# Three edits to the order of background work in a retention and two-layer MLP kernel

## The chip, the cores and the metric

The kernel runs on one core of a Trainium2 chip. Its engines work side by side, each through its own queue in order: TensorE (PE, matmuls into PSUM banks), VectorE (DVE), ScalarE (ACT), GpSimd (POOL), and SyncE (SP), which here only issues DMAs. The metric is the time of one execution on the device in microseconds (us), the median of several runs.

## What is computed

A retention layer over 4 batches, 8 heads, 768 steps and head size 64, then two MLPs on 3072 tokens of width 512 with a hidden width of 2048:

```python
def _attn_ref(q, k, v) -> np.ndarray:
    ...
    for t in range(S):
        state = gamma[None, :, None, None] * state + np.einsum('bhd,bhe->bhde', k[:, :, t], v[:, :, t])
        y[:, :, t] = scale * np.einsum('bhd,bhde->bhe', q[:, :, t], state)
    return y.astype(np.float32)
...
    h = x @ w_in
    g = np.maximum(0.01 * h, h)
    return (g @ w_out).astype(np.float32)
...
    h = x @ w_in
    g = h - np.tanh(h)
    return (g @ w_out).astype(np.float32)
```

The second MLP takes the first one's output. Weights and results keep more precision than one fp32r matmul gives: each operand is split into a high part (`xch`, `gh`, `wg`, rounded by ScalarE in `upper`) and a low part (`xcl`, `gl`, what is left, subtracted by VectorE in `lower`), and three matmuls (high x high, high x low, low x high) stand for one product.

## The kernel before

**Stages.** The retention comes first. Then the first MLP's input product runs as a stream of 168 products: the tokens go in three pairs of blocks (`sb`), and each of the 8 column groups `g` of a pair takes seven products P1 to P7 of 2 x 2 sub-blocks (the sums and differences of a fast matrix product) instead of eight. A product is six matmuls of 128x512. Its input forms of the activations are B11, B21, T1, T2, B22, T3 and T4, made in `build_xc` from the stored activations `x1s`; the weights' seven forms per group come from `form_sets`. Results are joined (`c`), rectified and stored in DRAM as `g1s`.

Then the outer steps: step `o` takes one 128-row piece of the hidden activations (loaded into `gr`, split into `gh` and `gl`) and adds its product with `w_out` to four PSUM banks, 12 matmuls a step, 16 steps for a block of 512 tokens. At the end of a block `evac` copies the four banks out on ScalarE (`st`, L692) and two ticks later they are stored in `x2s`. The first 48 outer steps (three blocks) run alone, in the loop over `ND_FROM`. After that the second MLP's input products (`Xd`, `Yd`, `Zd`, `prod`, 168 of them) are interleaved with the outer steps that are left, six matmuls in turn; a product's weight form `wf` is loaded from `wfs` four products ahead. The second MLP's own outer steps end the program. The blocks use banks 4 to 7, except that the second and the last use banks 0 to 3.

**Order of the work around it.** The order is written by hand: the program is emitted in one go, and `tick` counts emitted units of TensorE's work. Background work stands in queues of generators: `conv` converts the weights from float64 (`Convert`: load `raw`, one ScalarE step, four VectorE steps), `bg` and `forms` build weight forms, `bx` builds activation forms, `loads` loads activations. `run` takes from these queues as much work as a budget of estimated microseconds allows: 1.3 a product in the first stream, 1.85 an outer step in the loop over `ND_FROM`. A generator that yields `None` waits; `settle()` waits for the next tick. The converted second-layer weights become eight sets of forms (`form_d`); each set needs 16 free buffers before it starts, takes seven of them for its result, and `put_forms` stores them in `wfs` with seven DMAs, L299 and L301. A converted output weight is stored in `w2s` by `store2` (L271).

All SBUF buffers of this kind come from one pool of 94, first in, first out: `alloc` takes the one that was given back longest ago, and `give` returns a buffer as soon as its last reader is emitted. So the next writer of a buffer may have to wait for a DMA that still reads it. `defer(n, f)` puts off `f` by `n` ticks, and `flush` runs what is due, from the head of the list.

In the first stream `upper_g` and `lower_g` split the first outer activations around the last four products, and step 0 of the outer steps is emitted one product before the stream's end.

Of the kernel before, what the change touches and what calls it, by code (L numbers as in the profile page):

```python
# [14 lines left out]
AF = mybir.ActivationFunctionType  # L15
# [4 lines left out]
P = 128  # L20
NB, NH, NS, ND = 4, 8, 768, 64
# [4 lines left out]
NM = DFF // P  # L26
# [25 lines left out]
W2_EARLY, SLOT_US, W2_US, G_AHEAD = 8, 1.3, 1.2, 6  # L52
# [15 lines left out]
SPAN = 7 * NG  # L68

ND_FROM, N_TAIL, UNIT_US = 3 * NM, 28, 1.29  # L70
C_AHEAD, M_AHEAD, F_AHEAD, F_LOW, STORE_LAG = 6, 4, 4, 5, 3


@with_exitstack
def kernel(
# [12 lines left out]
    nc = tc.nc  # L88
# [13 lines left out]
    x2s = dr.tile([NC, NK, P, TB], F32, tag="x2s", name="x2s")  # L102
# [9 lines left out]
    def alloc(nm, dt=F32, shape=(P, TB)):  # L112
        pool, tag = free.popleft()
        serial[0] += 1
        t = pool.tile(list(shape), dt, tag=tag, name=f"{nm}_{serial[0]}")
        home[id(t)] = (t, pool, tag)
        return t

    def give(*ts):
        for t in ts:  # L120
            _, pool, tag = home.pop(id(t))
            free.append((pool, tag))
# [3 lines left out]
    now, tick = [-1], [0]  # L126

    def run(queues, us):

        while us > 0:  # L130
            for queue in queues:
                cost = next(queue[0], "end") if queue else None
                if cost is not None:
                    break
            if cost is None:
                return 0.0
            if cost == "end":
                queue.popleft()
            else:
                us -= cost  # L140
        return us

    def settle():

        t = tick[0]
        while tick[0] == t:
            yield None

    post = []

    def defer(n, f):
        post.append((tick[0] + n, f))

    def flush(all_=False):
        while post and (all_ or post[0][0] <= tick[0]):
            post.pop(0)[1]()

    def split(hi, lo, src, eng):

# [133 lines left out]
    forms = deque()  # L293
# [58 lines left out]
    one = Side(x1s, lambda sb, by: now[0] >= SPAN * sb - 7 + PROD[by][3])  # L352
# [19 lines left out]
    def build_xc(side, sb, part, done=None):  # L372
        while sb not in side.q:
            yield None
        q = side.q[sb]
        b11, b12, b21, b22 = q["B11"], q["B12"], q["B21"], q["B22"]

        def minus(eng, out, x, y):
            for kt in range(2):
                eng.tensor_tensor(out=out[kt], in0=x[kt], in1=y[kt], op=ALU.subtract)  # L380


        todo = (("B11", b11, "P1", None), ("B21", b21, "P2", (nc.vector, b11, b12, b11)), ("T1", b11, "P5", None),
                ("T2", b11, "P6", None), ("B22", b22, "P3", (nc.vector, b12, b22, b12)), ("T3", b12, "P7", None),
                ("T4", b21, "P4", None))
        for nm, src, by, nxt in todo[slice(*PARTS[part])]:
            while sb and not side.ready(sb, by):
                yield None
            if sb:
                for t2 in side.c[sb - 1].pop(nm):  # L390
                    give(*t2)
            while len(free) < 8:
                yield None
            if nm == "T2":
                minus(nc.vector, b11, b22, b11)
                yield 1.3
            if not sb and nm in ("T1", "T2"):
                yield from settle()
            out = [(alloc("xch", F32R), alloc("xcl", F32R)) for _ in range(2)]
            for kt in range(2):  # L400
                upper(out[kt][0], src[kt])
            yield from settle()
            for kt in range(2):
                lower(*out[kt], src[kt])
                yield 0.7
            side.c.setdefault(sb, {})[nm] = out
            if nxt:
                minus(*nxt)
                yield 1.3 if nxt[0] is nc.vector else 0.0
            if nm == "T3":  # L410
                minus(nc.vector, b21, b11, b21)
                yield 1.3
        if done:
            done()
# [7 lines left out]
    with tc.tile_pool(name="at", bufs=2, reuse_waits="tile") as at, \  # L422
# [168 lines left out]
        conv = deque([conversion(conv_in)])  # L591
        bg = deque([build_xc(one, 0, 0), build_wg(0), build_xc(one, 0, 1), build_wg(1), build_xc(one, 0, 2, free_x)])
        us = 0.0
# [12 lines left out]
        for s in range(len(steps)):  # L606
# [14 lines left out]
            if s >= CONV_FROM:  # L621
                us = run((conv, bg) if s % 2 else (bg, conv), min(us + ATT_US, ATT_US))
# [10 lines left out]
    NT = NC * NM  # L633
    GR, G, ACC, WE = {}, {}, {}, {}
# [9 lines left out]
    def load_g(o):  # L644
        if o < 2 * NT:
            nb, m = where_g(o)
            assert o < NT or (nb, m) in made2, (nb, m)
            GR[o] = alloc("gr")
            nc.sync.dma_start(out=GR[o], in_=(g1s if o < NT else g2s)[nb, m])  # L649

    def upper_g(o):
        if o < 2 * NT:
            G[o] = alloc("gh", F32R), None
            upper(G[o][0], GR[o])

    def lower_g(o):
        if o < 2 * NT:
            G[o] = G[o][0], alloc("gl", F32R)
            lower(*G[o], GR[o])
            give(GR.pop(o))  # L660
# [24 lines left out]
    def evac(o, half):  # L685
        if o % NM < NM - 1:
            return
        nb = where_g(o)[0]
        for j in (2 * half, 2 * half + 1):
            st = alloc("st")  # L690
            if o < NT:
                nc.scalar.activation(out=st.rearrange("p (a b) -> p a b", a=8),  # L692
                                     in_=ACC[j].rearrange("p (b a) -> p a b", a=8), func=AF.Copy)
                out_to = x2s[nb, j]
            else:
                if o == 2 * NT - 1 and j % 2:
                    nc.vector.tensor_copy(st, ACC[j])  # L697
                else:
                    nc.scalar.activation(out=st, in_=ACC[j], func=AF.Copy)
                r0 = j * NS + nb * P  # L700
                out_to = out[r0:r0 + P, :]

            def put(st=st, out_to=out_to):
                nc.sync.dma_start(out=out_to, in_=st)
                give(st)

            if o == 2 * NT - 1:
                put()
            else:
                defer(2, put)  # L710

    def step(o):
        for half in range(2):
# [72 lines left out]
    bx = deque(build_xc(one, sb, part) for sb in range(1, NSB) for part in range(3))  # L786
    loads = deque(load_xq(one, sb, lambda at=SPAN * (sb - 1) + 38: now[0] >= at) for sb in range(1, NSB))
    xleft = [(c, p) for c in range(2, NC) for p in range(NPAIR)]
    us = 0.0
    for i, (at_, sb, g, nm) in enumerate(stream):  # L790
        an, bn, bk, _ = PROD[nm]
        while g not in WG or bn not in XC.get(sb, {}):
            tick[0] += 1
            run((loads, bg, bx, conv), 0.01)
        product(sb, g, nm)
        now[0] = at_
        tick[0] += 1
        done, late[:] = late[:], []
        used = collect(sb, g, nm)
        for args in done:  # L800
            rectify(*args)
        if sb == NSB - 1 and nm == "P4":
            give(*WG[g][1])
        if xleft:
            c, p = xleft.pop(0)
            t = xw.pop((c, p))
            nc.sync.dma_start(out=x1s[c, p], in_=t)
            give(t)
        us = run((loads, conv, bg, bx) if not sb and at_ >= BG_FIRST and at_ % 2 == 0 else (loads, bg, bx, conv), min(us + SLOT_US - used, SLOT_US))
        if len(stream) - 8 <= i < len(stream) - 8 + G_AHEAD:  # L810
            load_g(i - len(stream) + 8)
        if len(stream) - 4 <= i < len(stream) - 1:
            upper_g(i - len(stream) + 4)
        if len(stream) - 3 <= i < len(stream) - 1:
            lower_g(i - len(stream) + 3)
        if i == len(stream) - 2:
            step(0)
    for t2 in XC[NSB - 1].values():
# [51 lines left out]
    def load_x0():  # L870
        q = {}
        for nm, kh, th in (("B11", 0, 0), ("B21", 1, 0), ("B12", 0, 1), ("B22", 1, 1)):
            while at_n[0] < (th + 1) * NM + 1:
                yield None
            q[nm] = [alloc("xq") for _ in range(2)]
            for i in range(2):
                nc.sync.dma_start(out=q[nm][i], in_=x2s[th, 2 * kh + i])
        arrive = tick[0] + LOAD_LEAD
        yield 0.0
        while tick[0] < arrive:  # L880
            yield None
        two.q[0] = q
# [7 lines left out]
    for n in range(ND_FROM):  # L890
        load_g(n + C_AHEAD if n + C_AHEAD < ND_FROM + M_AHEAD else 2 * NT)
        if n == 0:
            upper_g(3)
            lower_g(2)
            continue
        while n % NM not in WO:
            tick[0] += 1
            run((conv,), 0.01)
        step(n)
        at_n[0] = n  # L900
        upper_g(n + 3)
        lower_g(n + 2)
        if ND_FROM - F_AHEAD <= n:
            load_f(n - ND_FROM + F_AHEAD)
        tick[0] += 2
        flush()
        us = run((loads, bx, forms, conv), min(us + 1.85, 1.9))


    events = {}  # L910
# [266 lines left out]
```

## Time and profile before

| | us |
|---|---|
| median of 3 runs | 1083.74 |
| lowest and highest run | 1082.7 and 1086.09 |
| the profiled execution | 1087.43 |
| its span, first to last instruction | 1085.7 |
| PE busy in the span | 1056.3 (97%) |
| DVE busy in the span | 824.1 (76%) |
| ACT busy in the span | 702.6 (65%) |

Busy time is the time in which an engine had at least one instruction in work; matmuls are pipelined, so a busy TensorE starts a 128x512 matmul every 0.215 us although one lasts 0.38 us. The shares are means over very different stages: what a stage loses is seen in a view of that stage alone.

### The profile page before, as it was taken

What the parts mean: (1) busy time and instruction counts of PE and PEld (TensorE: products, weight loads), DVE (VectorE), ACT (ScalarE), POOL (GpSimd) and SP (SyncE); (2) the same over time, 40 slices, a digit from 0 to 9 for tenths busy, and PEclk for the clock granted to TensorE, in tenths of its full rate; (3) what the DMA queues carried; (4) which work ended last, traced back from release to release, by engine and by line L of the source; (5) the groups of instructions that cost most, each with busy time, mean ns of one, the idle gap of its engine ahead of it and who ended that gap; (6) DMA issues with size and microseconds to landing.
All of it is one profiled execution on the core that took longest, in us unless ns stands there. A gap on an engine that the chain in (4) does not pass through costs nothing. (4 is left out here: it accounts for less than half of the span.)

```text
span 1085.7 us, 17570 instructions
## 1 busy us (share of the span) xinstructions
PE 1056.3 (97%) x5931; PEld 912.6 (84%) x5931; DVE 824.1 (76%) x1363; ACT 702.6 (65%) x1251; POOL 91.5 (8%) x124
## 2 busy tenths in 40 slices
PE   9999889999999999999999889999999999999998
PEld 6888778888888888888888778888888888888887
DVE  3578887675787968978888679989788988767730
ACT  4666576665676546656677478978668866676530
POOL 3231000000000000001110000111011011101000
PEclk9999999999999999999999989999999999999999
DMA  9997465485467869969997998999998888887641
GB/s 226 261 259 194 142 228 194 159 286 215 174 233 262 281 233 387 388 242 289 306 291 243 285 309 282 265 287 276 274 305 235 246 256 247 250 245 221 201 146 39
DMA packets 208634, 267.67 MB, mean 247 GB/s; under 512 B 65056, under 2 KB 106144, under 8 KB 208544
## 3 DMA queue, kind: packets, MB, share of 16 engines
q1 hardware_dynamic: 197888, 247.52, 68.5%
q0 software_dynamic: 10368, 18.88, 10.1%
q8 instruction: 47, 0.77, 0.3%
q14 instruction: 43, 0.35, 0.1%
q10 hardware_dynamic: 288, 0.15, 0.0%
HBM read 161.63 MB, written 85.98 MB: 228 GB/s over the span
## 5 line engine op out<-in xcount | busy, mean ns | idle before, releaser
L679 PE MATMUL o<-gh,wo 128*128 128x512 f32 x768 | 241.6, 382 | 1.8 <-ACT st L692 1.8
L169 ACT ACTIVATE gh<-gr 128x512 fp32r<-128x512 f32 x192 | 118.0, 623 | 78.3 <-DMA gr<-g1s 37.1
L679 PEld LDWEIGHTS o<-gh,wo 128*128 128x128 f32 x768 | 146.3, 191 | 23.1 <-ACT st L692 2.2
L679 PE MATMUL o<-gl,wo 128*128 128x512 f32 x384 | 147.2, 383 | 8.4 <-DVE gl L175 8.3
L175 DVE TENSOR_TENSOR gl<-gr,gh 128x512 fp32r<-128x512 f32 x192 | 130.2, 685 | 26.9 <-ACT gh L169 23.4
L679 PE MATMUL o<-w2h,gl 128*128 128x512 f32 x384 | 145.5, 379 | 0.0
L679 PE MATMUL o<-w2h,gh 128*128 128x512 f32 x384 | 145.5, 379 | 0.0
L679 PE MATMUL o<-w2l,gh 128*128 128x512 f32 x384 | 145.5, 379 | 0.0
L1018 PE MATMUL Xd<-xch,wf 128*128 128x512 f32 x384 | 130.9, 383 | 3.8 <-ACT kp L920 3.8
L998 POOL DMA_DIRECT2D et<-h x72 | 62.0, 862 | 855.6 <-DMA wf<-wfs 415.5
L746 PE MATMUL X<-xch,wg 128*128 128x512 f32 x384 | 123.5, 381 | 4.1 <-DVE wg L175 1.8
L985 DVE COPY_PREDICATED es<-mk,et 128x512 f32<-128x512 uint16 x96 | 71.1, 744 | 46.6 <-ACT mk L959 46.5
L679 PEld LDWEIGHTS o<-gl,wo 128*128 128x128 f32 x384 | 73.2, 191 | 21.1 <-DVE gl L175 10.7
L746 PEld LDWEIGHTS X<-xch,wg 128*128 128x128 f32 x384 | 72.4, 189 | 16.9 <-DVE wg L175 2.6
L1018 PEld LDWEIGHTS Xd<-xch,wf 128*128 128x128 f32 x384 | 73.4, 191 | 14.8 <-ACT kp L920 4.2
L679 PEld LDWEIGHTS o<-w2h,gh 128*128 128x128 f32 x384 | 72.6, 189 | 10.3
L679 PEld LDWEIGHTS o<-w2l,gh 128*128 128x128 f32 x384 | 72.6, 189 | 10.3
L679 PEld LDWEIGHTS o<-w2h,gl 128*128 128x128 f32 x384 | 72.6, 189 | 10.3
L947 ACT ACTIVATE eu<-h 128x512 f32<-128x512 f32 x96 | 59.8, 623 | 28.6 <-DVE h L927 24.2
L746 PE MATMUL X<-xcl,wg 128*128 128x512 f32 x192 | 73.2, 381 | 1.5 <-DVE xcl L175 1.4
L963 DVE SCALAR_TENSOR_TENSOR ew<-eu,h 128x512 f32<-128x512 f32 x96 | 65.8, 685 | 10.5 <-ACT eu L947 4.6
L1018 PE MATMUL Xd<-xcl,wf 128*128 128x512 f32 x192 | 73.4, 382 | 0.0
(100 smaller groups left out, 2028.4 us busy)
## 6 DMA issues: line engine op xcount, KB each, us to landing
wf<-wfs SPq DMA_DIRECT2D x168, 256.0 KB, 4.4
g1s<-c SPq DMA_DIRECT2D x96, 256.0 KB, 2.1
gr<-g1s SPq DMA_DIRECT2D x96, 256.0 KB, 5.5
g2s<-es SPq DMA_DIRECT2D x96, 256.0 KB, 3.6
gr<-g2s SPq DMA_DIRECT2D x96, 256.0 KB, 4.1
et<-h POOLq DMA_DIRECT2D x72, 256.0 KB, 5.5
raw<-in_moe_w_in_dram SPq DMA_DIRECT2D x32, 512.0 KB, 5.8
raw<-in_moe_w_out_dram SPq DMA_DIRECT2D x32, 512.0 KB, 4.7
```

What stands on the lines that cost most here:

```text
L169: nc.scalar.activation(out=hi, in_=src, func=AF.Copy)
L175: nc.vector.tensor_tensor(out=lo, in0=src, in1=hi.bitcast(F32), op=ALU.subtract)
L679: nc.tensor.matmul(ACC[j], a, il(b), start=first and i == 0, stop=last and i == 2)
L746: nc.tensor.matmul(ps, w[:, c], il(x), start=first and kt == 0 and i == 0, stop=kt == 1 and i == 2, skip_group_check=True)
L947: nc.scalar.activation(out=e["u"], in_=h, func=AF.Square)
L963: nc.vector.scalar_tensor_tensor(out=e["w"], in0=e["u"], scalar=C3, in1=h, op0=ALU.mult, op1=ALU.mult)
L985: nc.vector.copy_predicated(out=e["s"], mask=e["mk"].bitcast(mybir.dt.uint16), data=e["th"])
L998: nc.gpsimd.dma_start(out=e["th"], in_=h, accum_op=ALU.add)
L1018: nc.tensor.matmul(ps, a, il(b), start=nm in ("P1", "P2", "P5") and kt == 0 and j == 0, stop=kt == 1 and j == 2, skip_group_check=True)
```

## The change

Four things. The first two blocks' results (outer steps 15 and 31) are copied out of PSUM with a delay of five ticks, that is after the third step behind the block's last has been emitted, and with them their stores and the loads that read them back (three steps later). `flush` runs whatever is due, wherever it stands in the list. The budget of an outer step in the loop over `ND_FROM` goes from 1.85 to 2.0. In the stream, the first outer activations are loaded three products earlier, and rounded and subtracted two products earlier. In `build_xc`, the first MLP's forms no longer wait for the next tick between rounding and subtracting.

```diff
-C_AHEAD, M_AHEAD, F_AHEAD, F_LOW, STORE_LAG = 6, 4, 4, 5, 3
+C_AHEAD, M_AHEAD, F_AHEAD, F_LOW, STORE_LAG, EVAC_LAG = 6, 4, 4, 5, 3, 5
...
     def flush(all_=False):
-        while post and (all_ or post[0][0] <= tick[0]):
-            post.pop(0)[1]()
+        while post:
+            due = [x for x in post if all_ or x[0] <= tick[0]]
+            if not due:
+                return
+            for x in due:
+                post.remove(x)
+                x[1]()
...
             for kt in range(2):
                 upper(out[kt][0], src[kt])
-            yield from settle()
+            yield 0.0
+            if side is not one:
+                yield from settle()
             for kt in range(2):
                 lower(*out[kt], src[kt])
                 yield 0.7
...
         nb = where_g(o)[0]
-        for j in (2 * half, 2 * half + 1):
...
+        js = (2 * half, 2 * half + 1)
+        if o < 2 * NM:
+            for j in js:
+                defer(EVAC_LAG, lambda j=j, acc=ACC[j]: take_out(o, nb, j, acc))
+        else:
+            for j in js:
+                take_out(o, nb, j, ACC[j])
+
+    def take_out(o, nb, j, acc):
+        st = alloc("st")
...
-        if len(stream) - 8 <= i < len(stream) - 8 + G_AHEAD:
-            load_g(i - len(stream) + 8)
-        if len(stream) - 4 <= i < len(stream) - 1:
-            upper_g(i - len(stream) + 4)
-        if len(stream) - 3 <= i < len(stream) - 1:
-            lower_g(i - len(stream) + 3)
+        if len(stream) - 11 <= i < len(stream) - 11 + G_AHEAD:
+            load_g(i - len(stream) + 11)
+        if len(stream) - 6 <= i < len(stream) - 3:
+            upper_g(i - len(stream) + 6)
+        if len(stream) - 5 <= i < len(stream) - 3:
+            lower_g(i - len(stream) + 5)
...
-            while at_n[0] < (th + 1) * NM + 1:
+            while at_n[0] < (th + 1) * NM + 4:
...
-        us = run((loads, bx, forms, conv), min(us + 1.85, 1.9))
+        us = run((loads, bx, forms, conv), min(us + 2.0, 2.0))
```

`take_out` is the old body of the loop in `evac`. TensorE's and GpSimd's instructions stand in the same order before and after. Line numbers after `flush` move by 5 to 15.

On SP, shortly after the loads of the second pair's activations (`xq_B`) for the second MLP, the last set of weight forms was stored (L299, L301; `wf` loads a form, `gr` an outer activation):

```order
L364 DMA xq_B_6701<-x2s 128x2x512
L649 DMA gr_6710<-g1s 128x512
L991 DMA g2s<-es_6613 128x512
L864 DMA wf_6745<-wfs 128x512
L649 DMA gr_6749<-g1s 128x512
L864 DMA wf_6769<-wfs 128x512
L864 DMA wf_6799<-wfs 128x512
L299 DMA wfs<-wg_6682 128x2x256
...
L301 DMA wfs<-wg_6688 128x512
L649 DMA gr_6813<-g1s 128x512
```

In the changed kernel no form store stands behind the same loads:

```order
L369 DMA xq_B_6707<-x2s 128x2x512
L879 DMA wf_6716<-wfs 128x512
L656 DMA gr_6726<-g1s 128x512
L1006 DMA g2s<-es_6641 128x512
L879 DMA wf_6762<-wfs 128x512
L656 DMA gr_6767<-g1s 128x512
L879 DMA wf_6788<-wfs 128x512
L879 DMA wf_6814<-wfs 128x512
L656 DMA gr_6824<-g1s 128x512
```

The last set stands some 100 rows further up in SP's queue, among the loads for the second MLP's first products:

```order
L202 DMA raw_1_5581<-in_moe_w_out_dram 128x1024
L276 DMA w2s<-cv_5459 128x512
L879 DMA wf_5591<-wfs 128x512
L879 DMA wf_5626<-wfs 128x512
L656 DMA gr_5634<-g1s 128x512
L304 DMA wfs<-wg_5506 128x2x256
...
L306 DMA wfs<-wg_5512 128x512
L879 DMA wf_5675<-wfs 128x512
```

So the store of the eighth set, behind 47 loads of `wf` before, stands behind 12 of them now.

On VectorE, at the turn from the second token pair to the third in the first stream (`c` joins two products of group `g` of the old pair, the number behind X, Y or Z being `g`; `xcl` is the low half of an activation form of the new pair, the third pair of them that of T1), there stood:

```order
L759 TENSOR_TENSOR c_3194<-Z_7_3187,P_280_3185 128x512
L759 TENSOR_TENSOR c_3213<-X_6_3106,P_275_3133 128x512
L175 TENSOR_TENSOR xcl_3216<-xq_B_3104,xch_3215 128x512
L175 TENSOR_TENSOR xcl_3218<-xq_B_3104,xch_3217 128x512
L759 TENSOR_TENSOR c_3239<-Y_7_3196,P_288_3227 128x512
L175 TENSOR_TENSOR xcl_3242<-xq_B_3124,xch_3241 128x512
L175 TENSOR_TENSOR xcl_3244<-xq_B_3124,xch_3243 128x512
L380 TENSOR_TENSOR xq_B_3104<-xq_B_3145,xq_B_3104 128x512 x2
L759 TENSOR_TENSOR c_3278<-Z_0_3271,P_295_3267 128x512
L175 TENSOR_TENSOR xcl_3281<-xq_B_3104,xch_3280 128x512
L175 TENSOR_TENSOR xcl_3283<-xq_B_3104,xch_3282 128x512
```

and now:

```order
L774 TENSOR_TENSOR c_3165<-Y_6_3128,P_277_3155 128x512
L180 TENSOR_TENSOR xcl_3188<-xq_B_3075,xch_3187 128x512
L180 TENSOR_TENSOR xcl_3190<-xq_B_3075,xch_3189 128x512
L774 TENSOR_TENSOR c_3202<-Z_7_3195,P_280_3185 128x512
L180 TENSOR_TENSOR xcl_3205<-xq_B_3095,xch_3204 128x512
L180 TENSOR_TENSOR xcl_3207<-xq_B_3095,xch_3206 128x512
L385 TENSOR_TENSOR xq_B_3075<-xq_B_3117,xq_B_3075 128x512 x2
L774 TENSOR_TENSOR c_3231<-X_6_3108,P_275_3135 128x512
L180 TENSOR_TENSOR xcl_3244<-xq_B_3075,xch_3243 128x512
L180 TENSOR_TENSOR xcl_3246<-xq_B_3075,xch_3245 128x512
```

T1's pair stood behind the first join of the new pair (Z_0) and now stands two joins of the old pair earlier, behind X_6.

On VectorE, at the end of the first stream, the first outer activation's low half (`gl`) stood behind the last group's second join (Y_7), with a converted weight's split (`wo`) just ahead of it:

```order
L759 TENSOR_TENSOR c_3975<-Y_7_3922,P_405_3959 128x512
L212 SCALAR_TENSOR_TENSOR cv_3916<-raw_1_3851,cv_3916 128x512
L215 SCALAR_TENSOR_TENSOR cv_3916<-raw_1_3851,cv_3916 128x512
L175 TENSOR_TENSOR wo_3997<-cv_3916,wo_3996 128x512
L175 TENSOR_TENSOR gl_4004<-gr_3920,gh_3980 128x512
L759 TENSOR_TENSOR c_4012<-X_7_3898,P_399_3929 128x512
```

and now:

```order
L217 SCALAR_TENSOR_TENSOR cv_3887<-raw_1_3823,cv_3887 128x512
L220 SCALAR_TENSOR_TENSOR cv_3887<-raw_1_3823,cv_3887 128x512
L774 TENSOR_TENSOR c_3961<-X_6_3814,P_388_3849 128x512
L180 TENSOR_TENSOR wo_3966<-cv_3887,wo_3965 128x512
L180 TENSOR_TENSOR gl_3985<-gr_3891,gh_3971 128x512
L774 TENSOR_TENSOR c_3993<-Y_7_3940,P_412_3979 128x512
```

It moved ahead of the join of Y_7 and of one weight unit's last steps.

## Rows read from the trace of the kernel before

**Rows 1.** Stretches: length; busy PE, PEld, DVE, ACT, POOL; clock, DMA share, GB/s.

```profile
116.00:160.00 44.00, 38.38 (x168) 30.56 (x167) 40.85 (x79) 30.32 (x56) 0.00 (x0) 1.00 0.65 221
...
352.00:474.00 122.00, 122.00 (x567) 106.81 (x567) 101.81 (x180) 67.33 (x117) 0.00 (x0) 1.00 0.86 302
420.00:460.00 40.00, 40.00 (x187) 35.02 (x186) 38.04 (x69) 25.44 (x46) 0.00 (x0) 1.00 1.07 388
...
596.00:640.00 44.00, 36.06 (x145) 29.95 (x145) 29.67 (x49) 24.63 (x46) 3.90 (x5) 0.88 0.87 287
640.00:1080.00 440.00, 440.00 (x2041) 385.29 (x2040) 333.34 (x524) 299.53 (x528) 45.13 (x53) 1.00 0.80 239
776.00:792.00 16.00, 16.00 (x76) 14.01 (x75) 11.38 (x18) 10.33 (x20) 0.86 (x1) 1.00 1.00 347
```

**Rows 2.** ACT's and DVE's longest waits, 352 to 474 us: total, times, longest.

```profile
ACT st L692 <- PE o L679: 15.2, 3, 7.1
DVE wg L175 <- ACT wg L169: 10.3, 3, 8.2
```

**Rows 3.** TensorE's waits, 116 to 160 us.

```profile
PE X L746 <- DVE wg L175: 1.8, 2, 1.2
PE Y L746 <- DVE xcl L175: 1.8, 1, 1.8
...
PE X L746 <- DVE xcl L175: 0.5, 1, 0.5
PE X L746 <- ACT xch L169: 0.4, 1, 0.4
```

**Rows 4.** TensorE's waits, 160 to 300 us.

```profile
PE Y L746 <- DVE xcl L175: 1.0, 1, 1.0
PE X L746 <- ACT xch L169: 0.9, 2, 0.5
PE X L746 <- DVE xcl L175: 0.9, 2, 0.5
```

**Rows 5.** Timeline of TensorE: start, us, instruction, idle before and its releaser.

```profile
346.75 0.48 PE L679 MATMUL o<-gl,wo 128*128 128x512 f32 x1 [1.82 <-DVE gl L175]
617.41 0.80 PE L679 MATMUL o<-gl,wo 128*128 128x512 f32 x1 [3.80 <-DVE gl L175]
631.80 0.79 PE L1018 MATMUL Xd<-xch,wf 128*128 128x512 f32 x1 [3.80 <-ACT kp L920]
```

**Rows 6.** TensorE's waits, 474 to 596 us.

```profile
PE o L679 <- DVE gl L175: 2.7, 2, 1.7
PE o L679 <- ACT st L692: 1.8, 1, 1.8
```

**Rows 7.** Chain that ended last, 590 to 640 us: start, us, what.

```profile
598.53 0.43 SPq L364
...
600.58 6.64 DMA g2s<-es
...
607.28 7.61 DMA wf<-wfs
...
623.18 5.72 DMA gr<-g1s
```

**Rows 8.** SP's waits, 596 to 632 us; the third row 486 to 504.

```profile
SPq L271 <- DVE cv L215: 5.6, 1, 5.6
SPq L864 <- DVE wg L177: 5.4, 1, 5.4
...
SPq L864 <- DMA wfs<-wg: 5.0, 1, 5.0
```

**Rows 9.** Timeline of SP: start, us, the form stores issued in a row.

```profile
617.15 4.61 SPq L299 DMA_DIRECT2D wfs<-wg  x6
```

**Rows 10.** Timelines of ScalarE and VectorE, as in rows 5.

```profile
611.07 0.63 ACT L169 ACTIVATE gh<-gr 128x512 fp32r<-128x512 f32 x1 [7.47 <-DMA g2s<-es]
...
499.92 0.69 DVE L963 SCALAR_TENSOR_TENSOR ew<-eu,h 128x512 f32<-128x512 f32 x1 [1.43 <-DMA wfs<-wg]
```

More of the change, by code (lines that the diff above doesn't have):

```diff
@@ L688, in evac, with put @@
         nb = where_g(o)[0]
-        for j in (2 * half, 2 * half + 1):
[L690 to L694, printed above, removed]
-            else:
[L696 to L710, printed above, removed]
+        js = (2 * half, 2 * half + 1)
[7 more added lines that the diff above has]
+        st = alloc("st")
+        if o < NT:
+            nc.scalar.activation(out=st.rearrange("p (a b) -> p a b", a=8),
+                                 in_=acc.rearrange("p (b a) -> p a b", a=8), func=AF.Copy)
+            out_to = x2s[nb, j]
+        else:
+            if o == 2 * NT - 1 and j % 2:
+                nc.vector.tensor_copy(st, acc)
+            else:
+                nc.scalar.activation(out=st, in_=acc, func=AF.Copy)
+            r0 = j * NS + nb * P
+            out_to = out[r0:r0 + P, :]
+        def put(st=st, out_to=out_to):
+            nc.sync.dma_start(out=out_to, in_=st)
+            give(st)
+        if o == 2 * NT - 1:
+            put()
+        else:
+            defer(2, put)
     def step(o):
```

## Prediction

> **What bounds the kernel now.** I read first the busy time by stretches. TensorE has the same 4320 large matmuls to run whatever the other engines do, so a gain can only come from stretches where it does not run them back to back. From 352 to 474 us, the first outer steps, it is busy for 122.00 of 122 us and starts 567 matmuls, 0.2152 us each (2.58 us for an outer step of 12); from 640 to 1080 us it is busy for all 440 [rows 1]. So the block ends inside 352 to 474 us cost TensorE nothing, although ScalarE stands there for 15.2 us in three waits (up to 7.1) for TensorE's last step before it can copy a block out, and VectorE waits 10.3 us for ScalarE [rows 2]: both run far enough ahead. The losses lie elsewhere, and the waits of TensorE name who was late:
> - 116 to 160 us: 5.6 us idle [rows 1], behind splits of the first activations (1.8, 0.5 and 0.4 us) and behind weight sets (1.8) [rows 3].
> - 160 to 300 us: 1.0 + 0.9 + 0.9 = 2.8 us, all behind the splits for the second and third token pair [rows 4].
> - 346.75 us: 1.82 us behind the first `gl`, the low half of the first outer activation [rows 5].
> - 474 to 596 us: 2.7 + 1.8 = 4.5 us [rows 6].
> - 596 to 640 us: the largest. 44 us hold 44/122 x 567 = 204 matmuls, 145 ran; 59 x 0.2152 = 12.8 us are lost. Of these 7.9 are idle (44 - 36.06), mostly two waits of 3.80 us [rows 1, 5]; the other 4.9 are matmuls run at a mean granted clock of 0.88, the two levels being 1.2 and 2.4 GHz.
>
> **Why 596 to 640 us stalls.** The chain of waits goes through DMAs: a store of `es` takes 6.64 us to release a buffer, a load of `wf` 7.61, and later a load of `gr` 5.72 [rows 7]. Two things meet there. Four loads of the next activations, 512 KB each, flood the DMA engines from 598.53 us on [rows 7]; and the last of the eight sets of second-layer weight forms is only now being built, because its builder asks for 16 free buffers and the pool has long been nearly empty. SP takes its queue in order, so it stood 5.6 us before a store of a converted weight and 5.4 us before a buffer that the last form's VectorE subtraction had to release; then it issued seven form stores in a row from 617.15 us, and the `gr` load behind them came at 623.18 [rows 7 to 9]. ScalarE waited 7.47 us for its activation meanwhile [rows 10].
>
> **The change, part by part**, against the profiled execution's own 1087.43 us (span 1085.7). TensorE's and GpSimd's programs are the same before and after, so each term is a wait.
>
> (1) More background work per outer step (2.0 instead of 1.85). By the code's own order, 5 of the 8 form sets were stored before the second layer's first product, and now 7 with it; the last set's stores stood behind the 47th `wf` load and now stand behind the 12th. Between the four big loads at 598 us and the next block end no form or conversion is left on SP, and on VectorE and ScalarE the eight steps of the last set go away from there. What is late next? The four big loads stay. Their twin, for the third token pair, is in the trace: 776 to 792 us, 347 GB/s, DMA share 1.00, and TensorE is busy for 16.00 of 16 us [rows 1]. There no form set is under way; that is what after will look like. Bounds for this term: 0 and -12.8. I take **-12.0**, by the twin.
>
> Its price: the last set now lands near 495 us. Where the seventh did, just before that, SP waited 5.0 us for form stores to release a buffer, and VectorE 1.43 us in one of three such waits; TensorE lost 1.0 (2.7 less the 1.7 of a later one) [rows 6, 8, 10]. The same set of waits comes a little later with the pool as empty or emptier. Bounds: -1.0 (the old wait goes and no new one comes) and +5.0 (SP's wait lands whole on TensorE). I take **+1.0**, nearer to what a set cost in the same stretch.
>
> VectorE's load in the outer stage: 38.04 of 40 us busy at 420 to 460 [rows 1]. 40 us are 15.5 steps, 0.15 more each is 2.3 us: 40.3, just full. Cover: it runs ahead of TensorE, as the waits for TensorE show. Cost 0; if the cover were gone, some 0.3 us per 40 us, below 1 us in the stage.
>
> (2) Copies of the first two blocks three steps later. ScalarE no longer waits at those two ends (at the third it still does, that copy is not deferred). TensorE waited for none of it: 0. Banks: the next user of the first block's banks is a block (16 steps) away, so no wait is added. The second block's stores and the loads that read them move three steps as well, 7.7 us, and the splits of the second layer's first activations with them; they are still emitted ahead of the products that read them, the tightest by some 30 matmuls (6.5 us). Cost 0, +1 if VectorE is late there.
>
> (3) First outer activations loaded, rounded and split two or three products earlier (a product is 6 x 0.2152 = 1.29 us). The first `gl` moves ahead by two products, 2.6 us, with a weight split just ahead of it as before; the wait was 1.82. **-1.8**, bounds 0 and -1.8.
>
> (4) Splits of the first layer without the pause of a product between rounding and subtracting. For the second and third pair the splits now stand up to four products before their use, where the first waits were for those emitted at the use itself: **-2.8**, bounds -1.4 and -2.8. In 116 to 160 us VectorE is busy for 40.85 of 44 us [rows 1], so there work has to go, not only move: by the order some 3 us of conversion steps move out of the first 120 matmuls. The 0.5 and 0.4 go, since the last split moves ahead by three products; of the 1.8 behind weight sets and the 0.9 us not shown I take half; the 1.8 of the first wait stays, since four conversion steps are still ahead of the second half of that split. Together **-2.0**, bounds +1 and -3.8.
>
> (5) The other 3.5 us of 474 to 596 us: one wait is a block end (1.8), unchanged; one hung on late loads (1.7), with one or two weight units fewer in work. **-0.6**, bounds +3 and -3.5.
>
> Sum: -12.0 + 1.0 - 1.8 - 2.8 - 2.0 - 0.6 = -18.2; 1087.43 - 18.2 = 1069.2. The profiled execution is 3.7 above the median of the three timed runs (1083.74) and 1.3 above the highest. If all of that is the profiler's, the median becomes 1065.5; if it is a deeper stall at 596 us than usual, there is 3.7 less to win there, and it becomes 1069.2. I take the middle, **1067**.
>
> **Rivals.**
> (a) The big loads alone hold the stall: for it, they are what fills the DMA queues in the chain; against it, the twin at 776 us. Only half of 12.8 goes: 1067 + 6 = 1073.
> (b) The outer stage becomes bound by DMA: one form set more (7 x 256 KB) and the loads of its two weight units (2 x 512 KB) have to pass before 474 us, 2.8 MB; the stretch 420 to 460 us already moves 388 GB/s at a share of 1.07 [rows 1]. At that rate 2.8 MB are 7.3 us, and if the lead of the splits covers only 2 of them, 5 reach TensorE: 1072. Against it: 352 to 474 us as a whole moves 302 GB/s. The Trainium skill, DMA: Bandwidth & Descriptors, section Specifications, gives about 358 GB/s as one core's share of HBM; by that the stretch could not run as it does, and 2.8 MB would be 7.8 us, an estimate from that page. The row's 388 is above it, so the measured rate decides.
> (c) Slower: the stall is not removed but doubled near 480 to 510 us. The form sets at the second layer's start drain the pool to a few buffers; if each `wf`, `gr` and `ew` then takes a buffer whose form store is unfinished, both sets there cost what the one at 596 us did: +2 x 12.8 - 18.2 = +7.4, so 1091 by the median. It decides once TensorE's new waits between 474 and 520 us pass some 18 us. Against it: two sets were stored in that stretch before and cost 1.0.
> (d) The change does nothing measurable: earlier sets only trade one wait for another of equal size, 1084.
>
> **How the numbers follow.** Forecast 0.76 (1058 to 1072), (a) 0.09, (b) 0.06, (c) 0.05, (d) 0.04. Low end: all bounds at their best are -12.8 - 1.0 - 1.8 - 2.8 - 3.8 - 3.5 = -25.7, 1058 by the median. High end: (a) with the +5.0 of the new place instead of +1.0, 1077. Range 1058 to 1078. A measurement of this kernel can tell about 0.3% (3.3 us) from no change: faster 0.88, same 0.06, slower 0.06 (of (c), and 0.01 of all else).
>
> **What would show it.** In the trace after: no wait of 3 us or more of TensorE between 590 and 640 us and no stretch there below full clock (1); at most 2 us of waits around 490 to 510 us (1); no wait before the first `gl` near 340 us (3); none behind `xcl` or `xch` between 160 and 300 us (4); ScalarE's wait for TensorE at the first two block ends gone with no time won (2). I am wrong if TensorE waits inside 352 to 470 us, if a new wait near 500 us is longer than 6 us, or if the stall at 600 us returns with the four big loads alone.

## The result and the profile after

| | before | after |
|---|---|---|
| median of 4 runs, us | 1083.64 | 1064.57 |
| lowest and highest, us | 1082.7 and 1086.09 | 1063.71 and 1066.49 |
| the profiled execution, us | 1087.43 | 1064.45 |
| its span, us | 1085.7 | 1062.7 |

The ratio is 0.9823, 95% interval 0.9802 to 0.9844: 19.1 us faster. 1067 was forecast, in a range of 1058 to 1078. The busy times by stretches of after, with the columns of [rows 1]:

```profile
116.00:160.00 44.00, 40.24 (x183) 33.81 (x182) 39.79 (x74) 31.96 (x58) 0.00 (x0) 1.00 0.64 227
160.00:300.00 140.00, 138.07 (x636) 119.39 (x635) 102.45 (x173) 93.20 (x162) 0.00 (x0) 1.00 0.61 213
300.00:352.00 52.00, 51.96 (x241) 45.19 (x240) 44.79 (x74) 37.14 (x63) 0.00 (x0) 1.00 0.76 266
352.00:474.00 122.00, 121.98 (x566) 106.50 (x565) 107.25 (x194) 68.86 (x120) 0.00 (x0) 1.00 0.94 336
474.00:596.00 122.00, 120.68 (x557) 104.40 (x556) 108.81 (x179) 85.99 (x150) 14.91 (x17) 1.00 0.94 293
596.00:640.00 44.00, 44.00 (x206) 38.53 (x205) 35.41 (x56) 34.55 (x62) 5.17 (x6) 1.00 0.90 275
```

The same five stretches of before that show a loss, and the one that does not, had 168, 630, 233, 567, 540 and 145 matmuls. The differences (+15, +6, +8, -1, +17, +61), 0.2152 us each, are 3.2, 1.3, 1.7, -0.2, 3.7 and 13.1 us, together 22.8; TensorE's busy time before 116 us grows by 0.6 (114.03 against 113.40), and with it they make the difference of the spans, 23.0, to within 0.4. After 640 us TensorE is busy without a wait in both. Of the largest stall, [rows 5], nothing is left: 44.00 of 44 us, at a granted clock of 1.00. The four big loads of 512 KB are issued from 578.3 to 586.2 us now, some 20 us earlier than before; around them too TensorE is busy without a wait, for 60.00 of 60 us from 540 to 600 us.

What TensorE still waits for, first in 116 to 160, then in 160 to 300 us (columns as in [rows 3]):

```profile
PE Y L761 <- DVE xcl L180: 1.7, 1, 1.7
PE X L761 <- DVE wg L180: 1.3, 1, 1.3
PE X L761 <- DVE c L774: 0.4, 1, 0.4
PE Y L761 <- DVE wg L180: 0.3, 1, 0.3
...
PE X L761 <- DVE wg L180: 1.3, 1, 1.3
PE X L761 <- DVE c L774: 0.7, 2, 0.4
```

Where all waits of [rows 4] were for `xcl` and `xch`, none is left for them between 160 and 300 us; two new kinds, 2.0 us, stand for weight sets and joins. The only wait behind 352 us is where the eighth form set now lands: TensorE's wait, the set's stores on SP, and, from the chain of waits, a store of the set and ScalarE's copy of a product behind it (`h`; start, us, what):

```profile
503.68 0.48 PE L686 MATMUL o<-gl,wo 128*128 128x512 f32 x1 [1.32 <-DVE gl L180]
...
489.35 3.69 SPq L304 DMA_DIRECT2D wfs<-wg  x6
493.14 1.17 SPq L306 DMA_DIRECT2D wfs<-wg  x1
...
492.48 5.49 DMA wfs<-wg
...
498.06 0.61 ACT h L951
```

### The profile page after: what moved, and what is told of

Read it like the earlier page. It is cut to its first block, busy times and chain, and to the rows that moved or that the text cites. A ratio compares the mean times of both kernels' runs of the same rounds, so it can differ in the third digit from the quotient of the medians.

```text
span 1062.7 us, 17567 instructions
## 1 busy us (share of the span) xinstructions
PE 1049.6 (99%) x5931; PEld 910.0 (86%) x5931; DVE 825.9 (78%) x1363; ACT 706.6 (66%) x1251; POOL 92.2 (9%) x124
## 4 chain that ended last, share of the span: by engine, by line
PE 92%; DVE 3%; DMA 2%; ACT 1%; issue 1%; SPq 0%; DVEq 0%; ACTq 0%
PE o L686 46%; PE Xd L1033 11%; PE X L761 9%; PE Yd L1033 6%; PE Y L761 4%; PE Zd L1033 3%; PE sc L550 2%; PE y L572 2%; PE Z L761 2%; PE y L568 2%; PE kTp L515 1%; PE qTp L529 1%; PE u L589 1%; DMA x1s<-x 1%; DMA g1s<-c 1%
```

## Experiments: one edit taken out, or made alone

Every program runs TensorE's instructions in the same order. Two places, read from the order of the code, turn out to matter; they are counted in products of the second layer emitted: where the last converted output weight is stored in `w2s`, and where the eighth set is stored in `wfs`. The first of the four 512 KB loads stands at 36 or 37 everywhere; in time it is issued between 573 and 599 us. **Lead** is the time from the end of the subtraction that makes a step's `gl` on VectorE to the start of the first matmul that reads it on TensorE; the column is its mean over outer steps 70 to 74, around the first of the big loads. The last column is TensorE's matmuls from 596 to 640 us, as in [rows 1], 206 being no loss. Lead and matmuls are read from one profiled execution of each kernel, the median from at least four runs. For before that execution lies 3.8 us above the median; for the kernels with the budget at 1.85 again and with set and conversions held it was the fastest of four, 2.3 and 1.7 us below the median, so their usual loss is somewhat larger than the column says.

| kernel | median us | ratio to before, 95% | last `w2s` | 8th set | lead us | matmuls |
|---|---|---|---|---|---|---|
| before (1082.8 to 1083.8 by group of runs) | 1083.4 | 1 | 36 | 42 | 0.4 | 145 |
| after | 1064.6 | 0.9802 to 0.9844 | 31 | 7 | 1.6 | 206 |
| after, budget 1.85 again | 1068.4 | 0.9827 to 0.9894 | 31 | 42 | 2.1 | 188 |
| before + budget 2.0 | 1070.9 | 0.9846 to 0.9908 | 29 | 35 | 3.5 | 198 |
| before + splits without pause | 1065.4 | 0.9799 to 0.9854 | 30 | 35 | 3.0 | 206 |
| before + first activations earlier | 1081.8 | 0.9969 to 0.9994 | 36 | 42 | 0.4 | 151 |
| before + copies later | 1080.8 | 0.9968 to 0.9995 | 36 | 42 | 0.7 | 165 |
| after, set held | 1064.7 | 0.9791 to 0.9844 | 28 | 42 | 5.1 | 195 |
| after, set and conversions held | 1068.3 | 0.9832 to 0.9879 | 36 | 42 | 3.2 | 186 |
| after, conversions held | 1062.8 | 0.9783 to 0.9822 | 36 | 6 | 1.4 | 202 |
| set and conversions held, lead spent | 1074.8 | 0.9912 to 0.9941 | 36 | 42 | 0.1 | 166 |
| after, lead spent | 1069.0 | 0.9860 to 0.9890 | 31 | 7 | 0.2 | 206 |

**The budget.** The prediction put the whole stall on the larger budget. It was taken out of after, and made alone in before:

```diff
-        us = run((loads, bx, forms, conv), min(us + 2.0, 2.0))
+        us = run((loads, bx, forms, conv), min(us + 1.85, 1.9))
```

> The changed kernel with the budget of an outer step back at 1.85 (cap 1.9). By the code's order the eighth form set is then stored 42 products into the second layer, 4 products behind the first of the four 512 KB loads, as in the kernel before (7 products in after). Theory A (the set's stores among those loads make the stall; the larger budget took it away): the stall at 596 to 640 us returns, 9 to 13 us, so 1074 to 1078. Theory C (the stall went through another of the edits): 1064 to 1066.

> The kernel before with the larger budget alone. By the code's order the eighth set is stored 35 products in, one product (2.6 us) ahead of the first 512 KB load: not early, as in after (7), and not behind them, as before (42). Theory A (it has to land among the big loads): the greater part of the stall goes, 1071 to 1075. Theory B (a set that takes the last free buffers costs its 10 us wherever it lands once the pool is low): no gain, 1081 to 1085.

Alone it gains 12.7 us (1083.6 to 1070.9), what theory A said at its best. But taken out of after it costs only 3.8: less than theory A's least, more than theory C's most. TensorE lost there, at 596 to 640 us and in a part of it (`kp` is ScalarE's copy of a product out of PSUM):

```profile
PE Xd L1033 <- ACT kp L935: 1.9, 1, 1.9
...
596.00:640.00 44.00, 42.10 (x188) 36.16 (x187) 35.36 (x57) 33.77 (x62) 6.03 (x7) 0.96 0.95 292
613.00:617.00 4.00, 4.00 (x13) 3.16 (x12) 4.00 (x7) 4.00 (x9) 0.00 (x0) 0.59 0.90 290
```

The set lies behind the big loads again, at 42, and 18 matmuls are lost where before lost 61 (188, 145 and 206). So another edit takes most of the stall away as well.

**The splits.**

```diff
                 upper(out[kt][0], src[kt])
-            yield from settle()
+            yield 0.0
+            if side is not one:
+                yield from settle()
```

> The kernel before with the activation splits of the first layer without their pause, alone. TensorE's waits of 2.8 us at 160 to 300 us and some 2 us at 116 to 160 us go; and by the code's order the eighth set moves here too, to 35 products in, one ahead of the big loads. Theory A: 1083.7 - 4 - 9 to 12 = 1068 to 1071. Theory B: 1079 to 1081, the splits' own gain alone.

This one edit gives 18.2 of the 19.1 us, more than theory A allowed. Some 5 us of it lie where it works, ahead of the outer steps (its first outer matmul starts at 339.48 us, after's at 339.50, before's at 344.55); the rest is nearly all the stall at 596 us (206 matmuls, with one wait of 0.5 us just ahead of the stretch). A reason stands in the code: `run` returns 0 as soon as every queue has yielded `None`, so a builder that waits for the next tick can throw away what is left of a product's budget. Without the pause the conversions behind the first stream's background stand earlier (last store 30 instead of 36), and so does the set (35 instead of 42). The splits were not taken out of after, so what after would lose without them is not known.

**First activations and copies.** Each alone, on before:

```diff
-        if len(stream) - 4 <= i < len(stream) - 1:
-            upper_g(i - len(stream) + 4)
...
+        if len(stream) - 6 <= i < len(stream) - 3:
+            upper_g(i - len(stream) + 6)
...
```

```diff
...
+        if o < 2 * NM:
+            for j in js:
+                defer(EVAC_LAG, lambda j=j, acc=ACC[j]: take_out(o, nb, j, acc))
...
```

> The kernel before with the earlier first outer activations alone; forms and conversions stand where they stood before. The wait of 1.82 us before the first outer step goes, the stall at 596 to 640 us stays: 1083.6 - 1.8 = 1081.8, so 1081 to 1083.

> The kernel before with the first two blocks' copies three steps later, alone; the last conversion and the eighth set stand where they stood before. By the forecast it gains nothing: 1083 to 1085. Rival: ScalarE's freed time lets VectorE run ahead and the waits of 474 to 596 us go: 1080 to 1081.

The first activations give 1.6 us, as expected. The copies give 2.6, where nothing was forecast: the rival's size, but not its way, since at 474 to 596 us TensorE still waits (554 matmuls, against 561 with the first activations alone). Where the first activations alone ran 151 matmuls at 596 to 640 us, the copies alone ran 165 (first row: first activations; second: copies):

```profile
596.00:640.00 44.00, 37.62 (x151) 30.83 (x150) 30.20 (x50) 26.58 (x50) 5.17 (x6) 0.88 0.92 296
596.00:640.00 44.00, 37.67 (x165) 31.75 (x164) 32.63 (x54) 26.89 (x51) 5.16 (x6) 0.96 0.94 297
```

TensorE is busy for the same time, but less of it at the lower of its two levels (mean granted clock 0.96 against 0.88): 14 matmuls, 3.0 us. That is one profiled execution of each, while the 2.6 us are from 12 runs; that the gain comes by this way is not shown.

## Experiments: is it where the set lands?

After was given the late set back, then the late conversions with it, then the late conversions alone:

```diff
-        while len(free) < 16:
+        while len(free) < 16 or (len(formed) == NG - 1 and dnow[0] < 38):
```

```diff
...
+    LATE = {(1, 12): 12, (1, 5): 16, (1, 13): 19, (1, 6): 23, (1, 14): 27, (1, 7): 30, (1, 15): 33}
...
             if 1 <= n <= last:
+                while dnow[0] < LATE.get((units[n - 1].half, units[n - 1].m), -1) and units[n - 1] in conv2:
+                    yield None
...
```

> The changed kernel, in which only the eighth set is held back until 38 products of the second layer are emitted (stored at 42, as before); its conversions and all else stay as early as in after. Theory A: the stall returns in full without any change of the budget, 1074 to 1078. Theory C (the earlier conversions, not the set, took the stall away): 1064 to 1067.

> The changed kernel in which the eighth set is held as in the run with the held set, and the last seven conversions of output weights of the second layer as well, so that the last store in w2s stands directly ahead of the first 512 KB load, as before (36 products in; 31 in after). Theory D (the stall needs the late conversions, with the set behind the loads): it returns, 9 to 13 us, 1073 to 1078. Theory E (neither is the cause; the lead that the engines bring along, or another place in the pool of buffers, is): 1064 to 1067.

> The changed kernel with the same seven conversions held, the eighth set left early (stored 6 products in). Theory D1 (late conversions and big loads are enough): 1072 to 1076. Theory D2 (it takes the late set too): 1065 to 1068. Theory E: 1064 to 1067.

With the set held it is stored behind the big loads (SP: start, us, instruction), and TensorE waits 1.7 us:

```profile
596.10 4.64 SPq L304 DMA_DIRECT2D wfs<-wg  x6
600.78 1.30 SPq L306 DMA_DIRECT2D wfs<-wg  x1
...
PE o L686 <- ACT st L707: 0.9, 1, 0.9
PE Xd L1033 <- ACT kp L935: 0.8, 1, 0.8
```

The median is that of after, 1064.7: the stretch loses 11 matmuls (195 against 206), and 474 to 596 us, where the wait at 503.68 us is gone, gains 10 (567 against 557). Theory A fell with this run: a set that meets the big loads is not enough. Nor are the late conversions alone (theory D1): 1062.8 us, below all that was forecast and, if anything, faster than after. Both together cost 3.8 us against after, between what theories D and E allowed:

```profile
PE Xd L1035 <- ACT kp L937: 2.7, 1, 2.7
PE o L689 <- ACT st L710: 0.9, 1, 0.9
...
596.00:640.00 44.00, 40.37 (x186) 34.74 (x185) 34.24 (x55) 34.52 (x64) 5.17 (x6) 1.00 0.96 304
```

By the two places of the table the background work stands as it stood in before; 186 matmuls ran instead of 145. One thing that differs is what the engines bring along. In before VectorE's lead is 0.4 us on the mean of outer steps 70 to 74, here 3.2. Ahead of the wait of 3.80 us before `gl` [rows 5] the `gl` of two steps in a row (77 and 78), and the first matmul that reads the earlier one, are these, in before and then with set and conversions held (there the later one's reader too):

```profile
605.31 0.68 DVE L175 TENSOR_TENSOR gl<-gr,gh 128x512 fp32r<-128x512 f32 x1
616.67 0.68 DVE L175 TENSOR_TENSOR gl<-gr,gh 128x512 fp32r<-128x512 f32 x1
609.56 0.38 PE L679 MATMUL o<-gl,wo 128*128 128x512 f32 x1
...
590.47 0.68 DVE L180 TENSOR_TENSOR gl<-gr,gh 128x512 fp32r<-128x512 f32 x1
598.62 0.68 DVE L180 TENSOR_TENSOR gl<-gr,gh 128x512 fp32r<-128x512 f32 x1
597.05 0.38 PE L689 MATMUL o<-gl,wo 128*128 128x512 f32 x1
600.93 0.38 PE L689 MATMUL o<-gl,wo 128*128 128x512 f32 x1
```

TensorE needs 3.88 us from one step's `gl` to the next (600.93 - 597.05). In before VectorE made them 11.36 us apart, 7.5 us longer than that: a **blow** of 7.5 us. The lead was 609.56 - 605.99 = 3.6, and the wait is the difference, 3.9 (3.80 by the row). With set and conversions held they were 8.15 apart, a blow of 4.3, and the lead was 5.9: no wait at this place. Such a wait is **blow less lead**. That is a balance of times, which has to come out; what it tells is that the run differs from before in both, by 3.2 us in the blow and by 2.3 in the lead. In after, at the same two steps, the blow was 2.1 and the lead 7.8.

## Experiments: the lead spent

To test the lead by itself, VectorE was made to subtract 13 `gl` twice, in the kernel with set and conversions held, and in after:

```diff
             lower(*G[o], GR[o])
+            if 64 <= o < 77:
+                lower(*G[o], GR[o])
```

> The run with set and conversions held (1068.3), in which VectorE subtracts the low half `gl` of outer steps 64 to 76 twice (13 more instructions of 0.61 us, the same result). In that run the `gl` of steps 70 to 74 was done 2 to 4 us before TensorE read it, in the kernel before 0 to 1 us. Theory F (the blow, late set and late conversions at the big loads, is the same in both, and TensorE pays what exceeds this lead): the lead shrinks by some 3 us, and the stall at 596 to 640 us grows by 3 to 9 us: 1071 to 1077. Rival G (the lead does not matter): 1068 to 1070.

> The changed kernel with the same 13 doubled subtractions, set and conversions early. Theory F: the lead is spent, but no blow meets it: 0 to 3 us, 1064.6 to 1067.6, no wait above 2 us at 580 to 620 us. If spent lead alone makes the stall: 1070 and more. Rival G: 1064 to 1066.

The stretches 474 to 596 and 596 to 640 us, first with set and conversions held, then of after, both with the doubled subtractions:

```profile
474.00:596.00 122.00, 119.78 (x549) 102.87 (x548) 109.56 (x176) 81.83 (x143) 13.51 (x16) 1.00 0.86 256
596.00:640.00 44.00, 37.83 (x166) 31.88 (x165) 33.03 (x55) 28.75 (x53) 4.71 (x6) 0.96 0.97 311
...
474.00:596.00 122.00, 118.50 (x541) 101.23 (x540) 112.53 (x184) 83.74 (x146) 13.13 (x16) 1.00 0.91 279
596.00:640.00 44.00, 44.00 (x206) 38.53 (x205) 37.34 (x59) 35.70 (x65) 5.94 (x7) 1.00 0.96 299
```

In both the lead at steps 70 to 74 is gone (0.1 and 0.2 us), and TensorE pays for it in small waits before 596 us. Behind that they part: at step 77, the earlier of the two steps above, the lead is 1.6 us with the late set and conversions, and 5.2 again in after. With the late set and conversions the stall is there again, 166 matmuls (186 without the doubled subtractions), 1.4 us before a `gl` and then 4.0 before a `kp`; the third row is ScalarE's, ahead of that `kp`:

```profile
606.13 0.48 PE L691 MATMUL o<-gl,wo 128*128 128x512 f32 x1 [1.42 <-DVE gl L180]
...
620.26 0.48 PE L1037 MATMUL Xd<-xch,wf 128*128 128x512 f32 x1 [4.02 <-ACT kp L939]
...
617.45 0.63 ACT L174 ACTIVATE gh<-gr 128x512 fp32r<-128x512 f32 x1 [4.91 <-DMA gr<-g1s]
...
620.00:624.00 4.00, 3.74 (x10) 3.00 (x11) 3.80 (x8) 4.00 (x9) 0.00 (x0) 0.58 0.55 152
```

The longer of the two waits is thus not one for `gl`: ScalarE stood 4.91 us for a load of `gr`; in before it stood 5.33 us for one, ahead of TensorE's wait of 3.80 us for `kp` [rows 5]. The lead of ScalarE's copies was not measured.

With the set early, as in after, there is no stall: 206 matmuls. It cost 4.4 us where theory F gave 0 to 3. By the trace it is all spent ahead of the stretch (541 matmuls against after's 557 at 474 to 596 us); between 540 and 600 us VectorE is busy for 58.42 of 60 us. So of the 6.5 us that the doubled subtractions cost with set and conversions held (1068.3 to 1074.8), 4.4 are what they cost in after as well. The lead matters (rival G gave 1068 to 1070 and 1064 to 1066, both missed), and the 20 matmuls lost in the stretch in one run and none in the other bear theory F out in kind; by the medians only some 2 us speak for lead and blow together, over and above VectorE's extra work.

**What stays open.** The blow of before (7.5 us) was not made again: with set and conversions held it was 4.3, and 3.1 with the lead spent. In before ScalarE's activation in front of it waited 7.47 us [rows 10], with set and conversions held 2.90 us. Why the DMAs it hung on took longer in before was not tried. So the late set, the late conversions and a spent lead together lose 40 of the 206 matmuls, where before loses 61, or 55 with the first activations alone; what makes the rest is open. Nor do the runs say how the lead is lost between 474 and 560 us: over outer steps 56 to 63 it is 0.5 us in before, and 0.6 in after, which has no stall.

## Experiments: more of it

A budget of 2.4, and the late conversions with part of VectorE's early work on GpSimd:

```diff
-        us = run((loads, bx, forms, conv), min(us + 2.0, 2.0))
+        us = run((loads, bx, forms, conv), min(us + 2.4, 2.4))
```

```diff
...
             if nm == "T3":
-                minus(nc.vector, b21, b11, b21)
...
+                minus(nc.gpsimd if first else nc.vector, b21, b11, b21)
...
```

> The changed kernel with a budget of 2.4 an outer step instead of 2.0: by the code's order all eight sets are stored before the second layer's first product, and the last conversion 17 products in instead of 31. If VectorE's lead covers it, as the forecast says of 2.0, the wait of 1.3 us near 504 us goes and nothing else: 1062 to 1064. By VectorE's time: 47 steps in 352 to 474 us times 0.4 are 19 us more on 107 busy of 122, so VectorE is full before the stretch ends and TensorE waits some 3 to 6 us: 1066 to 1070. Rival of the forecast, DMA: the outer stage moves 336 GB/s in after; 6 MB more in it would fill it: 1068 to 1075.

> The run with the conversions held (1062.75), and two of the first pair's differences (those for T3 and T4) on GpSimd instead of VectorE, four instructions, at 116 to 170 us, where VectorE is busy for 40 of 44 us and TensorE still loses some 5 us. VectorE is relieved of 2.6 us there: if those waits are VectorE's load, 1 to 2.6 us less, 1060 to 1062; if GpSimd is late for T3 (its only reader is 5 products on), 1063 to 1065.

At 2.4 all sets are stored before the second layer starts and the lead at steps 70 to 74 is 5.5 us; the time is 1064.0 (0.9795 to 0.9836 of before), that of after. VectorE is busy for 116.10 of 122 us in the outer stage, and TensorE loses 0.8 us in it, behind a `gl`:

```profile
352.00:474.00 122.00, 121.24 (x562) 105.84 (x562) 116.10 (x210) 71.11 (x124) 0.00 (x0) 1.00 1.01 356
```

GpSimd's help gave nothing: 1062.75 (0.9795 to 0.9839), the same as the late conversions alone. At 116 to 160 us the wait of 1.3 us for a weight set became 0.6, and waits of 0.7 and 1.4 us for joins stand there instead of one of 0.4. The versions at 1062.8 us cannot be told from after: their intervals overlap.

## Why the prediction was right, and where it was not

**The basis.** The two readings left open, the profiler's cost or a deeper stall in the profiled execution of before, are decided: the profiled execution of after (1064.45) lies at the median (1064.57), and other timed runs of before itself went from 1080.5 to 1088.8. So before's extra 3.8 us were waits of that one execution, not the profiler's cost. They seem to have lain mostly where the prediction did not look for them, at 474 to 596 us: before with the first activations alone, in which the order of every engine's work is the same there, ran 561 matmuls in its profiled execution, before 540, that is 4.5 us more (one execution of each):

```profile
474.00:596.00 122.00, 121.02 (x561) 105.56 (x560) 110.45 (x183) 85.17 (x151) 13.28 (x15) 1.00 0.95 299
```

The traces differ by 23.0 us where 18.2 were worked out, the medians by 19.1 where 16.7 were forecast. The forecast of 1067 lies halfway between two readings of the same sum; the lower, 18.2 from the median, would have given 1065.5. That the time came out inside the range is in part luck: term (1) came out for another reason than the one given, and of the 4.8 us by which the traces differ more than the sum, 4.1 lie at 474 to 596 us, mostly, it seems, in waits of before's one profiled execution.

**(1) -12.0, measured -13.1: right in size, wrong in its cause.** (59 x 0.2152 is 12.7, not 12.8, and the stretch holds 206 matmuls, not 204.) The step "By the code's own order" counted the sets for the whole change and then booked their shift to the larger budget. The budget alone does bring 12.7 us, but without it the change keeps 15.2 of its 19.1, and the splits alone bring 18.2. The parts are not a sum: alone they make 18.2 + 12.7 + 2.6 + 1.6 = 35 us; the splits and the budget each remove the same stall. From 151 matmuls, with the first activations alone, to 206 it is 11.8 us. The step "Two things meet there", set and big loads, left out the rest: both met in the run with the set held, and TensorE waited 1.7 us; with the late conversions it waited 3.6, and with the lead spent as well 6.2, against 7.9 us idle in before.

**Its price and (5), +1.0 - 0.6, measured -3.7.** The wait where the set now lands is 1.3 us, as sized. But the block end "unchanged" at 1.8 us is gone, and so is the wait "on late loads". The step that failed is to take waits of one execution for the kernel's: with the first activations alone only one, of 1.0 us, was there, and with the copies alone three, of 2.0 us together, where before has 4.5. Measured from the row above the stretch gains nothing (561 against 557).

**(2) 0, measured alone -2.6.** Cover was read as "no wait of TensorE in the stage, so nothing to win". The lead that ScalarE and VectorE carry out of the stage does grow: over outer steps 40 to 47 it is 5.1 us in before, 11.4 with the copies alone and 12.1 in after. That this is what brings the 2.6 us is not shown: over steps 64 to 69 the lead is 1.7 us both in before and with the copies alone. In after ScalarE no longer waits at the first block end; at the second it waits longer than before (0.94 us), not less, and at the third too (7.14 us before):

```profile
422.60 0.60 ACT L707 ACTIVATE st<-o 128x512 f32<-128x512 f32 x1 [2.21 <-PE o L686]
464.04 1.18 ACT L707 ACTIVATE st<-o 128x512 f32<-128x512 f32 x2 [10.39 <-PE o L686]
```

That costs nothing: TensorE is busy for 121.98 of 122 us there. The longer ScalarE waits for TensorE, the further ahead it is.

**(3) -1.8, measured -1.7, alone -1.6.** Right.

**(4) -2.8 and -2.0, measured -1.3 and -3.2.** The sum is right (-4.5 for -4.8), the places are not: the 2.8 us of waits for splits went as said, but 2.0 us of new waits, for a weight set and joins, stand in that stretch. (The parts of the -2.0, 0.5, 0.4 and half of 1.8 + 0.9, make 2.25.) The "1.8 of the first wait" stayed, as said (1.7).

**The rivals.** (a) The big loads alone hold nothing: in after TensorE runs without a wait around them and behind them. (b) The outer stage took 336 GB/s without a wait, and 356 at a budget of 2.4 with 0.8 us lost; VectorE's cover held too. (c) The stall did not move to 480 to 510 us: 1.3 us against the 18 from which it would decide. Of the signs that the prediction named, one was not seen: ScalarE's wait at the second block end did not go, and the copies gained time.

## What to carry to other kernels

A wait of TensorE is a blow less the lead that the engines ahead of it bring to it: before blaming the transfers in the stall alone, measure from the timelines how long before its use each operand was ready in the steps ahead. An edit that is worth a few microseconds in its own stage (here a pause in a builder that forfeits its budget, some 5 us) can be worth several times that in a later one (18.2 us in all). Two edits may remove the same stall, so take each out of the finished version as well as adding each alone; here that was done for the budget only. One profiled execution can be some microseconds off the median: compare it with the timed runs before sizing terms from it.

## What the runs showed of the hardware that was not expected

A wait that is followed by the lower clock need not be the longest. With the budget of 1.85 TensorE waited 1.90 us and then ran 613 to 617 us at a mean granted clock of 0.59, most of it at the lower level (1.2 GHz), 13 matmuls instead of 18 or 19; with set and conversions held it waited 2.68 and 0.95 us and the stretch 596 to 640 us stayed at 1.00. The runs do not tell why. One core moved 356 GB/s over 122 us at a budget of 2.4, and 388 over 40 us in before [rows 1].
